# Second mixture of a fused attention and two-mixture kernel: ten weight quarters split ahead of time, kept in DRAM and fetched as parts

## The chip, the cores and the metric

The kernel runs on one core of a Trainium2 chip. The metric is device time in microseconds, the median of several runs. The engines are named as in the profile: PE is TensorE (matmul; PEld its weight loads), DVE is VectorE, ACT is ScalarE, POOL is GpSimd and SP is SyncE, which here only issues DMAs.

## The reference

Three stages follow each other. The third is the one that the change is about; the second is where the work goes.

```python
# 1: a chunked state-space attention over (4, 8 heads, 768, 32) gives x of 3072 tokens x 256
# 2: first mixture, 4 experts, every token through every expert
for e in range(4):
    h = np.maximum(x @ w1[e], 0.0)            # 256 -> 1024
    out += p[:, e:e + 1] * (h @ w2[e])        # 1024 -> 256
# 3: second mixture, 8 experts, each token goes to its best expert alone
expert_idx = np.argmax(x @ w_gate, axis=1)    # tokens gathered by expert into disp
h = np.maximum(np.einsum('ecd,edf->ecf', disp, w1), 0.0)
y = np.einsum('ecf,efd->ecd', h, w2)
out[i] = gate_w[i] * y[expert_idx[i], pos[i]]
```

## The kernel before

**Numbers in two parts.** Every fp32 weight and activation is split into a rounded high part and a low part (`fp32r`), and a product is three matmuls: high by high, high by low, low by high. A split is one ACT copy that makes the high part and one subtraction that makes the low part (`split_w`, L373; the copy is L379, the subtraction L380). Weights come from DRAM in quarters of 128 x 1024 (512 KB): quarters 0 and 1 are the halves of `w1`, quarters 2 and 3 those of `w2`.

**First mixture.** Tokens stand in seven blocks of 2, 3, 4, 4, 4, 4 and 3 times 128. For each block and expert, eight chunks f run: `up` (PE makes `ph`, ACT makes `hh` from it at L509, DVE makes `hl` at L510) and, two chunks later, `down`. Each such step ends in `tick`, which emits what is listed for that slot (`at_slot`), and then a share of the attention of the next block; there are 64 slots in a block of 32 chunks, so slot 2f follows `up` of chunk f. The attention's `mask` (L247) on DVE must be ready before PE's `products` (L255, L263, L291). POOL adds the experts' results (L557).

**Second mixture.** Expert e's tokens are gathered by DMA (`load_rows`, L696), turned on PE (`turn`, L703) and split (`turned`, L711 and L712). A set of branches that `choose` (L1082) makes picks an arm for each expert by its number of tokens: `narrow_program` (up to 256), one wide block (up to 384), or `full_program` (two blocks). Each arm runs `expert_block`: `up_part` makes `qh` on PE (L733 to L735), ACT makes `ring_hh` (L737) and DVE `ring_hl` (L738); `down_part` (L749, L750) adds up `yy`; at the end ACT and DVE scale it (L778, L779) and POOL scatters it to the output (L780). The first three chunks of expert e+1 (`head`; the third goes into a tile named `qs`) are the last thing in expert e's arm. `qh` has two buffers, so `up_part` of chunk 5 needs `ring_hl` of chunk 3 to be done.

**Weights of the second mixture.** Four sets of weight tiles serve eight experts, so set e+2 is filled while expert e runs. All of experts 0 to 2 is split in the last block of the first mixture, on POOL. In the arms of experts 1 to 5, `first_block` splits the four quarters of expert e+2 at slots 4, 6, 8 and 10, with the subtraction on DVE for quarters 1 and 2 and on POOL for 0 and 3; the raw quarter that takes the freed staging tile is loaded three slots later, five places ahead in the list `order`. A slot is a call of `go` in `expert_block`. In a narrow arm slots 1 to 3 come at once, slot 4 stands before chunk 3, and from there two slots belong to each chunk.

```python
        for c in range(4 if e + 2 < E2 else 0):
            m, i = (4, 6, 8, 10)[c], 4 * (e + 2) + c
            add(m, lambda w=order[i], lo=(nc.vector if c in (1, 2) else nc.gpsimd): split_w(2, *w, lo))
```

Each engine executes its own instructions in the order in which the program emits them, and waits at each for the semaphores of the others.

Of the kernel before, what the change touches and what calls it, by code (L numbers as in the profile page):

```python
# [8 lines left out]
F32 = mybir.dt.float32  # L9
F32R = mybir.dt.float32r  # L10
# [3 lines left out]
ALU = mybir.AluOpType  # L14
# [3 lines left out]
P = 128  # L18
# [4 lines left out]
DM = NH * HD  # L23
E1 = 4
E2 = 8
FF = 1024
# [43 lines left out]
def attention_moe_moe_kernel(ctx: ExitStack, tc: tile.TileContext, aps: dict, cap: int):  # L70
    nc = tc.nc
# [8 lines left out]
    sp = ctx.enter_context(tc.tile_pool(name="stage", bufs=3))  # L80
    hp_ = ctx.enter_context(tc.tile_pool(name="hidden", bufs=3))
    dp = ctx.enter_context(tc.tile_pool(name="scratch", bufs=1, space=bass.MemoryType.DRAM))
# [269 lines left out]
    late_pool = []  # L352
    W = {}

    def weight_src(moe, e, c):
        w1, w2 = aps[f"w1_{moe}"][e], aps[f"w2_{moe}"][e]
        if c < 2:
            return w1[P * c:P * c + P, :]
        return w2[512 * (c - 2):512 * (c - 2) + 512, :].rearrange("(f p) d -> p f d", p=P)

    def load_w(moe, e, c):
        if (moe, e, c) not in given:
            pool, n = (late_pool[0], 2) if moe == 2 and (4 * e + c) % 5 > 2 else (sp, 3)
            given[moe, e, c] = pool.tile([P, FF], F32, tag="stage", name=f"stg{moe}_{e}_{c}", bufs=n)
        st = given[moe, e, c]
        nc.sync.dma_start(st if c < 2 else st.rearrange("p (f d) -> p f d", d=DM), weight_src(moe, e, c))
    def weights(moe, e):
        w1 = [wp.tile([P, KD * FF], F32R, tag=n, name=f"{n}_{moe}_{e}") for n in ("w1h", "w1l")]
        w2 = wp.tile([P, 2, KD * FF], F32R, tag="w2", name=f"w2_{moe}_{e}")
        return [*w1, w2[:, 0], w2[:, 1], w2]  # L370


    def split_w(moe, e, c, lo):  # L373
        if (moe, e) not in W:
            W[moe, e] = weights(moe, e)
        h, l = W[moe, e][2 * (c // 2):2 * (c // 2) + 2]
        sl = slice(FF * (c % 2), FF * (c % 2) + FF)
        st = given[moe, e, c]
        nc.scalar.copy(h[:, sl], st)  # L379
        lo.tensor_tensor(l[:, sl], st, h[:, sl].bitcast(F32), ALU.subtract)  # L380
# [313 lines left out]
    def load_rows(e, k):  # L694
        base = e * cap_slots + k * SLOTS
        nc.sync.dma_start(place(e, k), disp[base:base + SLOTS, :].rearrange("(t p) d -> p t d", p=P))  # L696

    def turn(e, k):
        rows = place(e, k)
        t = [ps.tile([P, SLOTS], F32, tag="s", name=f"tr{e}_{k}_{d}", bufs=3) for d in range(KD)]  # L700
        for d in range(KD):
            for st in range(ST):
                nc.tensor.transpose(t[d][:, P * st:P * st + P], rows[:, st, P * d:P * d + P], ident)  # L703
        tp[e, k] = t
        nc.gpsimd.tensor_copy(gi[e, k], rows[:, :, DM:ROW])

    def turned(e, k):
        t = tp.pop((e, k))
        xh, xl = xs[e, k]
        for d in range(KD):  # L710
            nc.scalar.copy(xh[:, d], t[d])  # L711
            nc.vector.tensor_tensor(xl[:, d], t[d], xh[:, d].bitcast(F32), ALU.subtract)  # L712
# [95 lines left out]
    def hint(label):  # L808
        tc.mark_branch_hint_location(label, "LikelyTaken", engines=[mybir.EngineType.PE])
# [63 lines left out]
    for c in range(3):  # L873
        load_w(1, 0, c)
    loaded[2] = [load_decay(2, a_src, nc.sync), None, None, None]
    load_w(1, 0, 3)
    nc.gpsimd.memset(state, 0.0)
    clip_all()
# [21 lines left out]
    for c in range(4):  # L900
        load_w(1, 1, c)
# [14 lines left out]
    def at_slot(b, i, fn):  # L916
        wq.setdefault((b, i), []).append(fn)
# [28 lines left out]
        at_slot(0, i, lambda e=e, c=c: load_w(1, e, c))  # L946
    at_slot(0, 28, gating_loads)
    at_slot(0, 42, gating_setup)
    order = [(e, c) for e in range(E2) for c in range(4)]
    when = [18, 21, 24, 27, 34, 37, 40, 43, 50, 53, 56, 59]  # L950
    split_at(last, when[0:4], 2, 0)
    split_at(last, when[4:8], 2, 1)
# [29 lines left out]
    for i in range(len(seq) + LAG):  # L982
        if i < len(seq):
            b, e, f = seq[i]
# [53 lines left out]
    for i in range(5, len(order)):  # L1038
        e, c = order[i]
# [9 lines left out]
    def first_block(e, n, y, lead, two=False, over=None):  # L1049
        extra = {}  # L1050

        def add(i, fn):
            extra.setdefault(i, []).append(fn)

        if over:
            add(8, lambda: hint(over))
        if two:
            add(1, lambda: load_rows(e, 1))
            add(6, lambda: turn(e, 1))
            add(8, lambda: turned(e, 1))  # L1060
        if e + 1 < E2:
            add(1, lambda: load_rows(e + 1, 0))
            add(10, lambda: turn(e + 1, 0))
            add(12, lambda: turned(e + 1, 0))
        for c in range(4 if e + 2 < E2 else 0):
            m, i = (4, 6, 8, 10)[c], 4 * (e + 2) + c
            add(m, lambda w=order[i], lo=(nc.vector if c in (1, 2) else nc.gpsimd): split_w(2, *w, lo))
            if i + 5 < len(order):
                add(m + 3, lambda w=order[i + 5]: load_w(2, *w))
        expert_block(e, 0, n, extra, HEAD, early=(lead, y))  # L1070

    def second_into(e, tokens):
# [15 lines left out]
    def full_program(e, tokens, y):  # L1088
        first_block(e, SLOTS, y, LEAD, two=True)
        second_into(e, tokens)  # L1090
        head(e + 1)
        if e + 1 < E2:
            align(JOIN)

    def wide_programs(e, tokens, y, after):
        if nblk == 1:
            first_block(e, SLOTS, y, LEAD)
            head(e + 1)
            return
        choose(tokens <= SLOTS, f"full{e}", lambda: first_block(e, SLOTS, y, LEAD, over=f"next{e}"), None)  # L1100
        choose(tokens > SLOTS, f"next{e}", lambda: full_program(e, tokens, y), after)
# [85 lines left out]
```

## Time and profile before

| | |
|---|---|
| median of 3 runs | 780.46 us (779.81 to 781.44) |
| the profiled execution | 778.74 us |
| its span, first to last instruction | 776.9 us |
| granted TensorE clock, mean | 0.998 |
| PE busy | 759.9 us (98%) |
| DVE, ACT, POOL busy | 439.0, 284.4, 187.7 us |
| bytes moved by DMA | 82.52 MB |

The span is divided by the program's stages: the seventh block of the first mixture ends at about 602 us, expert 0 of the second mixture runs to 641 us, and experts 1 to 7 follow up to 771 us. In this data experts 1 and 3 take the wide arm, experts 2, 4, 5 and 6 the narrow one, expert 7 two blocks. Experts 2, 4, 5 and 6 thus run the same PE program, and expert 6 does it without any split beside it.

### The profile page before, as it was taken

The numbers are of one execution on the slowest core, as the hardware profiler recorded it, in microseconds if no ns is written. First come the engines' busy times: TensorE is split into PE (matmuls) and PEld (weight loads), VectorE is DVE, ScalarE is ACT, GpSimd is POOL, SyncE is SP. The second block draws the span as 40 slices with busy tenths as digits, with TensorE's granted clock in tenths as the row PEclk, the third lists the DMA queues.
The fourth block names the chain that finished last, engine by engine and source line by source line (L and its number), as shares of the span: only waits on it lengthen the run. The fifth ranks groups of instructions, "written<-read, shape, count | busy, mean of one in ns | idle before, by whom it ended". The sixth has DMA issues, their size and how long they took to land. (4 is left out here: it accounts for less than half of the span.)

```text
span 776.9 us, 12841 instructions
## 1 busy us (share of the span) xinstructions
PE 759.9 (98%) x4746; PEld 666.3 (86%) x4746; DVE 439.0 (57%) x872; ACT 284.4 (37%) x579; POOL 187.7 (24%) x227
## 2 busy tenths in 40 slices
PE   9999999999999999999999999999999999898996
PEld 7889999987888878888888888889999999797996
DVE  5785788456663576635676456553533545657432
ACT  1553443233332333323332333322444235456431
POOL 1010102212210132110321112111396215544411
PEclk9999999999999999999999999999999999999999
DMA  9763567623210232102322022131154204454000
GB/s 257 234 204 106 188 217 220 180 86 105 82 59 27 85 113 84 69 22 77 114 85 82 17 72 86 41 105 53 51 178 128 94 23 151 159 171 137 27 34 28
DMA packets 50195, 82.52 MB, mean 106 GB/s; under 512 B 5104, under 2 KB 35009, under 8 KB 50108
## 3 DMA queue, kind: packets, MB, share of 16 engines
q1 hardware_dynamic: 46340, 74.50, 30.2%
q0 software_dynamic: 2400, 6.11, 2.2%
q10 hardware_dynamic: 1368, 0.81, 0.5%
q8 instruction: 47, 0.77, 0.4%
q14 instruction: 40, 0.33, 0.1%
HBM read 65.56 MB, written 16.31 MB: 105 GB/s over the span
## 5 line engine op out<-in xcount | busy, mean ns | idle before, releaser
L510 DVE SCALAR_TENSOR_TENSOR hl<-ph,hh 128x512 fp32r<-128x512 f32 (+2 forms) x216 | 133.7, 619 | 232.6 <-ACT hh L509 228.9
L509 ACT ACTIVATE hh<-ph 128x512 fp32r<-128x512 f32 (+2 forms) x216 | 117.2, 543 | 344.0 <-PE ph L506 339.4
L504 PE MATMUL ph<-xh,w1h 128*128 128x512 f32 (+2 forms) x432 | 160.6, 372 | 0.7 <-DVE hl L510 0.7
L533 PE MATMUL acc<-hh,w 128*128 128x512 f32 (+2 forms) x432 | 158.0, 366 | 0.6 <-DVE x L549 0.5
L505 PE MATMUL ph<-xl,w1h 128*128 128x512 f32 (+2 forms) x432 | 156.4, 362 | 0.0
L506 PE MATMUL ph<-xh,w1l 128*128 128x512 f32 (+2 forms) x432 | 156.3, 362 | 0.0
L534 PE MATMUL acc<-hl,w 128*128 128x512 f32 (+2 forms) x432 | 156.3, 362 | 0.0
L535 PE MATMUL acc<-hh,w 128*128 128x512 f32 (+2 forms) x432 | 156.1, 361 | 0.0
L533 PEld LDWEIGHTS acc<-hh,w 128*128 128x128 f32 x432 | 81.2, 188 | 13.0 <-issue 1.4
L504 PEld LDWEIGHTS ph<-xh,w1h 128*128 128x128 f32 x432 | 81.2, 188 | 12.6 <-issue 2.4
L506 PEld LDWEIGHTS ph<-xh,w1l 128*128 128x128 f32 x432 | 81.2, 188 | 10.4
L535 PEld LDWEIGHTS acc<-hh,w 128*128 128x128 f32 x432 | 81.3, 188 | 10.4
L534 PEld LDWEIGHTS acc<-hl,w 128*128 128x128 f32 x432 | 81.3, 188 | 9.4
L505 PEld LDWEIGHTS ph<-xl,w1h 128*128 128x128 f32 x432 | 81.3, 188 | 8.7
L557 POOL TENSOR_TENSOR x<-x,cmb 128x512 f32<-128x512 f32 (+2 forms) x40 | 48.5, 1234 | 153.1 <-DVE cmb L554 153.0
L749 PE MATMUL yy<-w,ring_hh 128*128 128x512 f32 x208 | 76.4, 398 | 0.0
L738 DVE SCALAR_TENSOR_TENSOR ring_hl<-qh,ring_hh 128x384 fp32r<-128x384 f32 (+2 forms) x77 | 36.5, 476 | 55.9 <-ACT ring_hh L737 52.6
L750 PE MATMUL yy<-w,ring_hl 128*128 128x256 f32 x208 | 58.4, 281 | 0.0
L737 ACT ACTIVATE ring_hh<-qh 128x384 fp32r<-128x384 f32 (+2 forms) x77 | 32.9, 427 | 68.4 <-PE qh L735 66.6
L181 DVE TENSOR_TENSOR_SCAN lt<-abc,id 128x512 f32<-128x512 f32 x44 | 57.3, 1303 | 0.0
L733 PE MATMUL qh<-sxh,w1h 128*128 128x256 f32 (+2 forms) x126 | 39.0, 310 | 6.7 <-DVE ring_hl L738 6.4
L749 PEld LDWEIGHTS yy<-w,ring_hh 128*128 128x128 f32 x208 | 39.1, 188 | 6.2
(171 smaller groups left out, 996.1 us busy)
## 6 DMA issues: line engine op xcount, KB each, us to landing
stg<-in_w SPq DMA_DIRECT2D x34, 512.0 KB, 4.3
abc<-a_zero SPq DMA_DIRECT2D x21, 512.0 KB, 3.7
bcr<-in_bc SPq DMA_DIRECT2D x19, 512.0 KB, 3.8
disp<-zrow SPq DMA_DIRECT2D x12, 516.0 KB, 6.6
nat<-in_nat SPq DMA_DIRECT2D x24, 256.0 KB, 4.5
pb<-pT SPq DMA_DIRECT2D x16, 256.0 KB, 4.3
rw<-disp SPq DMA_DIRECT2D x10, 387.0 KB, 4.5
early_w<-in_w SPq DMA_DIRECT2D x6, 512.0 KB
```

The costliest lines, as they stand in the source:

```text
L181: nc.vector.tensor_tensor_scan(t["lt"][:, sl, :].rearrange("p h i -> p (h i)"), a_bc[:, sl, :].rearrange("p h i -> p (h i)"), id4.rearrang ...
L504: nc.tensor.matmul(ph[:, :n], lhsT=wh[:, c], rhs=xh[:, k, :n], start=k == 0, stop=False)
L505: nc.tensor.matmul(ph[:, :n], lhsT=wh[:, c], rhs=xl[:, k, :n], start=False, stop=False)
L506: nc.tensor.matmul(ph[:, :n], lhsT=wl[:, c], rhs=xh[:, k, :n], start=False, stop=k == KD - 1)
L509: nc.scalar.activation(hh[:, :n], ph[:, :n], AF.Relu)
L510: nc.vector.scalar_tensor_tensor(hl[:, :n], ph[:, :n], 0.0, hh[:, :n].bitcast(F32), ALU.max, ALU.subtract)
L533: nc.tensor.matmul(a[:, :n], lhsT=wh[:, c], rhs=hh[:, :n], start=f == 0, stop=False)
L534: nc.tensor.matmul(a[:, :n], lhsT=wh[:, c], rhs=hl[:, :n], start=False, stop=False)
L535: nc.tensor.matmul(a[:, :n], lhsT=wl[:, c], rhs=hh[:, :n], start=False, stop=f == NF - 1)
L557: (nc.vector if (b, e) == (last, experts(b)[-1]) else nc.gpsimd).tensor_tensor(dst[d], dst[d], tmp[d], ALU.add)
L749: nc.tensor.matmul(y, lhsT=hh[:, q], rhs=w2[:, :, c], start=j == 0, stop=False)
L750: nc.tensor.matmul(y[:, 0], lhsT=hl[:, q], rhs=w2[:, 0, c], start=False, stop=j == NF - 1)
```

## The change

Ten quarters (0 and 3 of experts 3 to 7, the list `apart`) are no longer loaded and split in the second mixture. In blocks 2 to 5 of the first mixture, three to a block, each is loaded, split in two halves of 512 columns (ACT copy, DVE subtraction in place) and its two parts are stored to the DRAM tile `parts`. In the arms of experts 1 to 5 four DMAs of 512 KB fetch the two parts of both quarters straight into the weight tiles at slot 2. The other two quarters are split at slots 4 and 7, both on DVE, and the raw loads follow two slots later; `order` now has 22 entries, so only the arms of experts 1, 2 and 3 still load raw quarters (2, 2 and 1 of them).

```diff
+    apart = [(e, c) for e in range(3, E2) for c in (0, 3)]
+    order = [(e, c) for e in range(E2) for c in range(4) if (e, c) not in apart]
+    parts = dp.tile([len(apart), 2, P, FF], F32, name="parts")
+    making = {}
+
+    def part_load(i):
+        making[i] = [sp.tile([P, FF], F32, tag="stage", name=f"raw{i}", bufs=3)]
+        st = making[i][0]
+        c = apart[i][1]
+        nc.sync.dma_start(st if c < 2 else st.rearrange("p (f d) -> p f d", d=DM), weight_src(2, *apart[i]))
+
+    def part_split(i, half):
+        if not half:
+            making[i].append(sp.tile([P, FF], F32R, tag="stage", name=f"high{i}", bufs=3))
+        st, h = making[i]
+        sl = slice(FF // 2 * half, FF // 2 * half + FF // 2)
+        nc.scalar.copy(h[:, sl], st[:, sl])
+        nc.vector.tensor_tensor(st[:, sl].bitcast(F32R), st[:, sl], h[:, sl].bitcast(F32), ALU.subtract)
+
+    def part_store(i):
+        st, h = making.pop(i)
+        nc.sync.dma_start(parts[i, 0], h.bitcast(F32))
+        nc.sync.dma_start(parts[i, 1], st)
+
+    def part_fetch(e, c):
+        sl = slice(FF * (c % 2), FF * (c % 2) + FF)
+        for k, w in enumerate(W[2, e][2 * (c // 2):2 * (c // 2) + 2]):
+            nc.sync.dma_start(w[:, sl].bitcast(F32), parts[apart.index((e, c)), k])
...
-    order = [(e, c) for e in range(E2) for c in range(4)]
+    for i in range(len(apart)):
+        b, s = 2 + i // 3, 16 * (i % 3)
+        at_slot(b, s + 2, lambda i=i: part_load(i))
+        at_slot(b, s + 20, lambda i=i: part_split(i, 0))
+        at_slot(b, s + 24, lambda i=i: part_split(i, 1))
+        at_slot(b, s + 27, lambda i=i: part_store(i))
...
         for c in range(4 if e + 2 < E2 else 0):
-            m, i = (4, 6, 8, 10)[c], 4 * (e + 2) + c
-            add(m, lambda w=order[i], lo=(nc.vector if c in (1, 2) else nc.gpsimd): split_w(2, *w, lo))
+            if (e + 2, c) in apart:
+                add(2, lambda c=c: part_fetch(e + 2, c))
+                continue
+            m, i = 3 * c + 1, order.index((e + 2, c))
+            add(m, lambda w=order[i]: split_w(2, *w, nc.vector))
             if i + 5 < len(order):
-                add(m + 3, lambda w=order[i + 5]: load_w(2, *w))
+                add(m + 2, lambda w=order[i + 5]: load_w(2, *w))
```

PE's instructions stand in the same order in both programs. Three places of the other engines show what moved.

DVE, the narrow arm of expert 2, before (`w1l`, `w` are the low parts of expert 4's weights, `stg` the raw quarters, `qh` chunks 3 to 7):

```order
L738 SCALAR_TENSOR_TENSOR ring_hl_6201<-qh_0_3_7576,ring_hh_6200 128x256
L380 TENSOR_TENSOR w1l_0_5657<-stg_3_0_6002,w1h_0_5656 128x1024
L738 SCALAR_TENSOR_TENSOR ring_hl_6205<-qh_0_4_7591,ring_hh_6204 128x256
L380 TENSOR_TENSOR w_2_0_5658<-stg_3_1_6085,w_2_0_5658 128x1024
L738 SCALAR_TENSOR_TENSOR ring_hl_6209<-qh_0_5_7607,ring_hh_6208 128x256
L738 SCALAR_TENSOR_TENSOR ring_hl_6201<-qh_0_6_7632,ring_hh_6200 128x256
```

The same arm after the change:

```order
L409 TENSOR_TENSOR w1l_0_5748<-stg_4_1_6203,w1h_0_5747 128x1024
L767 SCALAR_TENSOR_TENSOR ring_hl_6292<-qh_0_3_7665,ring_hh_6291 128x256
L767 SCALAR_TENSOR_TENSOR ring_hl_6296<-qh_0_4_7679,ring_hh_6295 128x256
L409 TENSOR_TENSOR w_2_0_5749<-stg_4_2_6235,w_2_0_5749 128x1024
L767 SCALAR_TENSOR_TENSOR ring_hl_6300<-qh_0_5_7694,ring_hh_6299 128x256
L767 SCALAR_TENSOR_TENSOR ring_hl_6292<-qh_0_6_7717,ring_hh_6291 128x256
```

The first subtraction has moved ahead of `ring_hl` of chunk 3; the second still stands ahead of chunk 5. POOL's two subtractions of this arm are gone.

SP, the narrow arm of expert 2, before (`rw` is the gathered rows of expert 3):

```order
L696 DMA rw_6196<-disp 128x3x258
L366 DMA stg_4_0_6169<-in_w_2 128x1024
L366 DMA stg_3_0_6002<-in_w_2 128x4x256
L366 DMA stg_3_1_6085<-in_w_2 128x4x256
L366 DMA stg_3_2_6112<-in_w_2 128x1024
L1082 UNCONDITIONAL_BRANCH x2
```

The same arm after the change:

```order
L725 DMA rw_6287<-disp 128x3x258
L388 DMA w1h_0_5747<-parts 128x1024
L388 DMA w1l_0_5748<-parts 128x1024
L388 DMA w_2_0_5749<-parts 128x1024 x2
L395 DMA stg_4_1_6203<-in_w_2 128x4x256
L395 DMA stg_4_2_6235<-in_w_2 128x1024
L1119 UNCONDITIONAL_BRANCH x2
```

Four fetches now stand behind the rows and ahead of two raw loads.

DVE, end of block 2 of the first mixture, before (`lt` is the attention's decay scan, `m` its masks, `cmb` the product with an expert's probability):

```order
L554 TENSOR_TENSOR cmb_3_1_2659<-acc_3_1_2480,pb_3_2276 128x512
L247 TENSOR_TENSOR m_2663<-sc_0_2648,lt_2635 128x512
L510 SCALAR_TENSOR_TENSOR hl_0_2_2673<-ph_0_2_2665,hh_0_2_2672 128x512
L181 SCALAR_TENSOR_TENSOR lt_2635<-abc_2506,id_87 128x512
L510 SCALAR_TENSOR_TENSOR hl_0_3_2702<-ph_0_3_2694,hh_0_3_2701 128x512
L247 TENSOR_TENSOR m_2705<-sc_1_2679,lt_2635 128x512
L510 SCALAR_TENSOR_TENSOR hl_0_4_2735<-ph_0_4_2727,hh_0_4_2734 128x512
```

The same place after the change:

```order
L583 TENSOR_TENSOR cmb_3_1_2680<-acc_3_1_2497,pb_3_2284 128x512
L247 TENSOR_TENSOR m_2684<-sc_0_2669,lt_2656 128x512
L539 SCALAR_TENSOR_TENSOR hl_0_2_2694<-ph_0_2_2686,hh_0_2_2693 128x512
L378 TENSOR_TENSOR raw_2462<-raw_2462,high_2697 128x512
L181 SCALAR_TENSOR_TENSOR lt_2656<-abc_2523,id_87 128x512
L539 SCALAR_TENSOR_TENSOR hl_0_3_2726<-ph_0_3_2718,hh_0_3_2725 128x512
L247 TENSOR_TENSOR m_2729<-sc_1_2703,lt_2656 128x512
L539 SCALAR_TENSOR_TENSOR hl_0_4_2759<-ph_0_4_2751,hh_0_4_2758 128x512
L378 TENSOR_TENSOR raw_2462<-raw_2462,high_2697 128x512
```

A half subtraction (`raw`) stands ahead of the second decay scan and so ahead of the second mask, and another behind chunk 4's `hl`.

## Rows read from the trace of the kernel before

**Rows 1.** The page's first part: busy time by engine.

```profile
PE 759.9 (98%) x4746; PEld 666.3 (86%) x4746; DVE 439.0 (57%) x872; ACT 284.4 (37%) x579; POOL 187.7 (24%) x227
```

**Rows 2.** Waits of PE, 600 to 777 us: total, times, longest.

```profile
PE qh L733 <- DVE ring_hl L738: 6.4, 5, 2.0
```

**Rows 3.** Timeline, DVE, second mixture: start, duration, instruction, idle before it.

```profile
661.12 0.96 DVE L738 SCALAR_TENSOR_TENSOR ring_hl<-qh,ring_hh 128x256 fp32r<-128x256 f32 x2 [0.37 <-ACT ring_hh L737]
...
668.40 3.35 DVE L380 TENSOR_TENSOR w<-stg,w 128x1024 fp32r<-128x1024 f32 x1
...
676.65 0.96 DVE L738 SCALAR_TENSOR_TENSOR ring_hl<-qh,ring_hh 128x256 fp32r<-128x256 f32 x2 [0.37 <-issue]
...
695.12 0.95 DVE L738 SCALAR_TENSOR_TENSOR ring_hl<-qh,ring_hh 128x256 fp32r<-128x256 f32 x2 [0.37 <-ACT ring_hh L737]
...
711.78 0.96 DVE L738 SCALAR_TENSOR_TENSOR ring_hl<-qh,ring_hh 128x256 fp32r<-128x256 f32 x2 [0.37 <-ACT ring_hh L737]
...
715.68 1.23 DVE L380 TENSOR_TENSOR w1l<-stg,w1h 128x1024 fp32r<-128x1024 f32 x1 [0.51 <-ACT w1h L379]
...
723.85 0.96 DVE L738 SCALAR_TENSOR_TENSOR ring_hl<-qh,ring_hh 128x256 fp32r<-128x256 f32 x2 [0.38 <-ACT ring_hh L737]
...
735.93 0.96 DVE L738 SCALAR_TENSOR_TENSOR ring_hl<-qh,ring_hh 128x256 fp32r<-128x256 f32 x2 [0.38 <-ACT ring_hh L737]
```

**Rows 4.** Timeline, POOL, second mixture.

```profile
668.30 2.37 POOL L380 TENSOR_TENSOR w<-stg,w 128x1024 fp32r<-128x1024 f32 x1
...
717.77 2.87 POOL L380 TENSOR_TENSOR w1l<-stg,w1h 128x1024 fp32r<-128x1024 f32 x1 [4.46 <-DMA rw<-disp]
```

**Rows 5.** Timeline, PE, chunks 5 and 7 of expert 2, chunk 5 of expert 4.

```profile
665.36 0.38 PE L733 MATMUL qh<-sxh,w1h 128*128 128x256 f32 x1
...
672.14 0.39 PE L733 MATMUL qh<-sxh,w1h 128*128 128x256 f32 x1 [1.94 <-DVE ring_hl L738]
...
700.48 0.39 PE L733 MATMUL qh<-sxh,w1h 128*128 128x256 f32 x1 [0.84 <-DVE ring_hl L738]
```

**Rows 6.** Timeline, ACT, third head chunk and first cast of experts 2, 4, 5, 6.

```profile
663.24 0.38 ACT L737 ACTIVATE ring_hh<-qs 128x256 fp32r<-128x256 f32 x1 [1.62 <-PE qs L735]
663.52 1.04 ACT L379 CAST w1h<-stg 128x1024 fp32r<-128x1024 f32 x1
...
698.02 0.39 ACT L737 ACTIVATE ring_hh<-qs 128x256 fp32r<-128x256 f32 x1 [2.40 <-PE qh L735]
698.64 1.05 ACT L379 CAST w1h<-stg 128x1024 fp32r<-128x1024 f32 x1 [0.24 <-issue]
...
713.38 1.05 ACT L379 CAST w1h<-stg 128x1024 fp32r<-128x1024 f32 x1
...
724.64 0.38 ACT L737 ACTIVATE ring_hh<-qs 128x256 fp32r<-128x256 f32 x1 [0.29 <-PE qs L735]
```

**Rows 7.** Groups by line and form, first 600 us: the subtraction of a quarter on DVE.

```profile
L380 DVE TENSOR_TENSOR w1l<-early_w1l,w1h 128x1024 fp32r<-128x1024 f32 x4 | 4.9, 1216 | 0.7 <-ACT w1h L379 0.5
```

**Rows 8.** Waits of PE, 130 to 600 us: the only row.

```profile
PE y L263 <- DVE m L247: 0.2, 1, 0.2
```

**Rows 9.** Timelines of POOL, DVE and PE at the end of block 2.

```profile
227.32 2.56 POOL L557 TENSOR_TENSOR x<-x,cmb 128x512 f32<-128x512 f32 x2 [19.70 <-DVE cmb L554]
...
223.84 1.21 DVE L181 TENSOR_TENSOR_SCAN lt<-abc,id 128x512 f32<-128x512 f32 x1
...
229.56 1.40 DVE L181 TENSOR_TENSOR_SCAN lt<-abc,id 128x512 f32<-128x512 f32 x1
231.94 0.69 DVE L510 SCALAR_TENSOR_TENSOR hl<-ph,hh 128x512 fp32r<-128x512 f32 x1 [0.98 <-ACT hh L509]
...
233.29 0.43 PE L263 MATMUL y<-m,nat 128*32 128x128 f32 x8 [0.19 <-DVE m L247]
```

**Rows 10.** Timeline of SP, expert 2's rows; windows, expert 1's four loads (last: DMA share, GB/s).

```profile
662.52 0.37 SPq L696 DMA_DIRECT2D rw<-disp  x1
...
652.00:660.00 8.00, 8.00 (x52) 7.43 (x51) 5.40 (x10) 4.16 (x9) 3.65 (x3) 1.00 0.77 258
```

More of the change, by code (lines that the diff above doesn't have):

```diff
@@ L359, in weight_src @@
         return w2[512 * (c - 2):512 * (c - 2) + 512, :].rearrange("(f p) d -> p f d", p=P)
+    apart = [(e, c) for e in range(3, E2) for c in (0, 3)]
[22 more added lines that the diff above has]
+            nc.sync.dma_start(w[:, sl].bitcast(F32), parts[apart.index((e, c)), k])
     def load_w(moe, e, c):
         if (moe, e, c) not in given:
-            pool, n = (late_pool[0], 2) if moe == 2 and (4 * e + c) % 5 > 2 else (sp, 3)
+            pool, n = (late_pool[0], 2) if moe == 2 and order.index((e, c)) % 5 > 2 else (sp, 3)
             given[moe, e, c] = pool.tile([P, FF], F32, tag="stage", name=f"stg{moe}_{e}_{c}", bufs=n)
```

## The prediction

> **What bounds the kernel now.** I read the page's first part first. PE is busy for 759.9 us of a span of 776.9 [rows 1], so no change that leaves PE's work alone can gain more than the remaining 17 us, and PE's instructions here stay in the same order. The next view is the list of PE's waits in the second mixture: 6.4 us in five waits, all of chunk matmuls for `ring_hl`, DVE's low part of an earlier chunk [rows 2]. In the middle of the first mixture, from 130 to 600 us, the same view has a single 0.2 us [rows 8]. The second mixture is thus where something can be won, and the first is where something can be lost.
>
> The timeline of DVE tells what the waits cost in all. Experts 2, 4, 5 and 6 run the same narrow PE program, and each begins with the pair of `ring_hl` of its head. From pair to pair expert 6, which splits nothing, takes 735.93 - 723.85 = 12.08 us; expert 5 takes 723.85 - 711.78 = 12.07; expert 2 takes 676.65 - 661.12 = 15.53 and expert 4 takes 711.78 - 695.12 = 16.66 [rows 3]. Experts 2 and 4 therefore lose 3.45 + 4.58 = 8.03 us. The wait list has 6.4 of it; the rest is in matmuls that restart slowly or run beside a missing operand.
>
> Why does expert 5 lose nothing, with the same four splits? Its DVE subtraction took 1.23 us, and POOL began its own only at 717.77, after it; in expert 2 POOL subtracted from 668.30 to 670.67, and DVE's subtraction that began at 668.40 lasted 3.35 us, to 671.75 [rows 3, 4]. Chunk 7 of expert 2 then waited 1.94 us for the `ring_hl` behind it [rows 5]. A quarter's subtraction on DVE with no POOL work beside it takes 1216 ns [rows 7]. So the loss is DVE's subtraction beside POOL's.
>
> **Second mixture: what is removed.** POOL's ten subtractions go, so no DVE subtraction runs beside one, and two of four ACT casts per arm go, 1.04 us each [rows 6]. For the stretch this leaves 1.22 us per subtraction. By that alone the whole 8.03 us would come back.
>
> **What is added there.** The first subtraction now stands ahead of `ring_hl` of chunk 3, and chunk 5 on PE needs that result. ACT casts first, so chunk 3's result is ready at the cast's end, plus 0.05 us to start, 1.22 for the subtraction and about 0.4 for `ring_hl` (a pair takes 0.96 with its gap [rows 3]). The cast begins when ACT has done the third head chunk, and here a row matters that has nothing to do with splits: that activation came 1.62 us late in expert 2 and 2.40 late in expert 4, where expert 6 has 0.29 [rows 6]. If ACT is as late again:
>
> - Expert 2: 663.52 + 1.04 + 0.05 + 1.22 + 0.4 = 666.2. Chunk 5 could start at 665.36 [rows 5, 6]. New wait 0.9 us.
> - Expert 4: 698.64 + 1.05 + 0.05 + 1.22 + 0.4 = 701.4. Chunk 5 started at 700.48 after a wait of 0.84, so it could have started at 699.64 [rows 5, 6]. New wait 1.75 us.
> - Expert 5: 713.38 + 1.05 + 0.05 + 1.22 + 0.4 = 716.1. Expert 2's chunk 5 stood 665.36 - 661.12 = 4.24 us behind its pair; the same offset here gives 711.78 + 4.24 = 716.0 [rows 3, 5, 6]. New wait 0.1 us.
>
> The second subtraction stands ahead of `ring_hl` of chunk 5, as before, has its cast no later than before, and takes 1.22 us where 3.35 us made chunk 7 wait 1.94; 1.94 is less than the 2.1 us saved, so nothing is left. Experts 1 and 3, in the wide arm, show no PE wait now, and PE has 384 columns per chunk to cover the same 1.22 us: nothing. Total: 8.03 - 0.9 - 1.75 - 0.1 = 5.3 us gained.
>
> **The fetches.** Four of 512 KB are 2.1 MB per arm; expert 1's four raw loads moved at 258 GB/s [rows 10], which makes 8.1 us. Expert 2's are issued behind the rows at 662.52 and first needed by expert 4's head just ahead of 695.12 [rows 3, 10], 32 us later; the last, in expert 5's arm, have more than 20. What covers them is the whole of the arm between. All six transfers and the rows are 3.5 MB and 13.7 us, more than a narrow arm of 12.1, but only experts 1 and 2 have six, and the rows that PE turns stand ahead of the fetches in SP's queue. Bounds: nothing, or 13.7 - 12.1 = 1.6 us once, if expert 3's arm finds its rows queued behind expert 2's loads. I take nothing, since expert 3 is wide and turns later.
>
> **First mixture: what is added.** Ten loads, twenty stores, twenty ACT copies and twenty DVE subtractions of 512 columns in blocks 2 to 5. Half of the quarter's price is 0.61 us, a DVE row of 512 columns has 0.69 [rows 7, 9]: 12 to 14 us of DVE in all, about 3.5 us per block. What hides it is DVE's idle time in front of each `hl`. The tightest place I found is the end of block 2: DVE's decay scan of 1.40 us ends at 230.96, then DVE stands idle for 0.98 us until ACT's `hh`, makes `hl`, then the second mask, and PE already waits 0.19 us for that mask [rows 9]. The new half stands ahead of the scan. 0.69 of the 0.98 us idle are used, and the mask is not later. If the cover were missing, the mask and PE would be late by the full 0.69 us. The same place comes back in blocks 3 and 4, so the bounds are 0 and 3 x 0.69 = 2.1 us. Elsewhere PE waits for neither masks nor `hl` today [rows 8]. I take 0.1 us. Stores and loads wait for work that was emitted slots before; ACT's copy of 0.52 us goes behind `hh`, where it delays only itself.
>
> POOL's adds at that place run until 227.32 + 2.56 = 229.88, and the half would begin at 229.56 [rows 9]. If it only shared with POOL, it would stretch as the scan did, 1.40 us against 1.21 for the scan before it, which had no POOL add beside it [rows 9]; if it had to wait for POOL's end, it would begin 0.32 late and end at 230.5 instead of 230.2, and a scan of 1.21 would end at 231.75, before 231.94. Both give nothing on the path. The Trainium skill (SBUF — State Buffer, section "Who interferes with whom") says that a DVE instruction with two SBUF inputs contends with a GpSimd instruction that reads SBUF, and that the loser blocks for the whole instruction; by that rule each half that meets a POOL add is late, and the sum is still unchanged as long as 0.98 us of idle time covers it.
>
> **Sum.** The profiled execution took 778.74 us, 1.7 us less than the median of the runs shown. 778.74 - 5.3 + 0.1 = 773.5. The same 5.2 us off the median of 780.46 give 775.3 us, a gain of 0.67%. A measurement of this kernel can tell about 0.2%, 1.6 us, from no change.
>
> **Rivals.**
>
> *ScalarE's lateness is not there.* It came in experts 2 and 4, both behind a wide arm, and not in expert 6. If it stays away, the three waits of 2.75 us vanish and the gain is 8.0: 772.4 us. Against it: nothing in the change is meant to touch it. Chance 0.18.
>
> *The lateness grows or spreads.* ACT was late by 1.62 and 2.40 us with no POOL or DVE work to wait for [rows 6]. If the new bursts of 2.1 MB at the start of each arm make ACT 1 us later in the three narrow arms, each us goes straight into chunk 5's wait, since the new order left no slack there: 3 us less gain, 778.3 us. Above 1.2 us each the change is lost in the noise. Chance 0.10. The Trainium skill (Runtime: NRT & Kernel Launch, section "Instruction fetch mechanics") says that a taken branch whose target lies outside the loaded window must fetch instructions by DMA before it goes on. By that rule the lateness is an instruction load, the new program has its pages elsewhere, and either this rival or the one before it would come true; no row here shows such a load as the cause.
>
> *Another wait takes the gain.* The rows or the fetches come late at two or three arms (1.6 us each by the bound above), and the time stays within 0.2%: 780 us. Against it, 32 us of cover. Chance 0.06.
>
> *Slower: the first mixture pays.* DVE's halves delay masks or `hl`. Each of the twenty costs at most 0.69 us, 13.8 us in all: 775.2 + 13.8 = 789 us. It decides from the point where they cost more than 5.2 + 1.6 = 6.8 us, so where at least ten of twenty come through. Against it: 0.2 us of PE waits in 470 us and DVE idle in front of nearly every `hl`; for it: a mask that PE waits for even now. Chance 0.06.
>
> **How the numbers follow.** My forecast, ACT as late as now, has 0.60 and a range of its own from 774 to 777 (half the lateness more or less, and the 2.1 us bound of the first mixture). 772.0 to 778.4 takes in the first two rivals and leaves out the last two, 0.12, and a little at the edges. Faster by over 0.2%: 0.60 + 0.18 + 0.10 = 0.88; within 0.2%: 0.06; slower: 0.06.
>
> **What would show it.** In the profile after: no POOL subtraction of 128x1024 behind 605 us; DVE's at 1.2 us each; expert 6's pair-to-pair time still 12.1 us, experts 2 and 4 at about 13 and 14; PE waits for `ring_hl` of 2 to 3 us, all at chunk 5; PE's waits from 130 to 600 us still under 0.5 us. I am wrong if PE waits for a DMA of `parts`, if masks in blocks 2 to 4 make PE wait by half a microsecond each, or if experts 2 and 4 stay above 15 us with short subtractions, which would say that ACT and not POOL made them late.

## The result, and the profile after

The changed kernel takes 770.79 us (median, 769.0 to 772.34) and the kernel before, beside it on the same chip, 780.13 (777.52 to 781.44): a ratio of 0.9879, 95% interval 0.9856 to 0.9901. I had said 775.3, with a range down to 772.0. The sign was right, the gain was 9.3 us in place of 5.2, and the time lies 1.2 us below the range. The profiled execution took 771.84 us, so from profile to profile the gain is 6.9 us.

The page's first part, to be held against [rows 1]:

```profile
PE 759.5 (99%) x4746; PEld 666.5 (87%) x4746; DVE 444.6 (58%) x892; ACT 286.3 (37%) x589; POOL 159.3 (21%) x217
```

PE's work is the same; 6.8 us of the span around it have gone. Waits of PE, first from 600 to 771 us, then from 130 to 600 us (total, times, longest):

```profile
PE qh L762 <- PEq L1119: 0.3, 1, 0.3
...
PE y L263 <- DVE m L247: 0.2, 1, 0.2
```

The 6.4 us for `ring_hl` of [rows 2] are gone, and the first mixture waits as before [rows 8]. The timeline of DVE, with the head pairs of experts 1 to 7 and the two subtractions of expert 2, answers to [rows 3]:

```profile
643.01 0.97 DVE L767 SCALAR_TENSOR_TENSOR ring_hl<-qh,ring_hh 128x256 fp32r<-128x256 f32 x2 [0.37 <-ACT ring_hh L766]
...
661.57 0.95 DVE L767 SCALAR_TENSOR_TENSOR ring_hl<-qh,ring_hh 128x256 fp32r<-128x256 f32 x2 [0.38 <-ACT ring_hh L766]
...
664.29 1.23 DVE L409 TENSOR_TENSOR w1l<-stg,w1h 128x1024 fp32r<-128x1024 f32 x1 [0.51 <-ACT w1h L408]
...
666.65 1.23 DVE L409 TENSOR_TENSOR w<-stg,w 128x1024 fp32r<-128x1024 f32 x1 [0.46 <-ACT w L408]
...
673.92 0.96 DVE L767 SCALAR_TENSOR_TENSOR ring_hl<-qh,ring_hh 128x256 fp32r<-128x256 f32 x2 [0.41 <-ACT ring_hh L766]
...
692.50 0.96 DVE L767 SCALAR_TENSOR_TENSOR ring_hl<-qh,ring_hh 128x256 fp32r<-128x256 f32 x2 [0.37 <-ACT ring_hh L766]
...
704.95 0.96 DVE L767 SCALAR_TENSOR_TENSOR ring_hl<-qh,ring_hh 128x256 fp32r<-128x256 f32 x2 [0.43 <-issue]
...
717.04 0.96 DVE L767 SCALAR_TENSOR_TENSOR ring_hl<-qh,ring_hh 128x256 fp32r<-128x256 f32 x2 [0.41 <-ACT ring_hh L766]
...
729.12 0.96 DVE L767 SCALAR_TENSOR_TENSOR ring_hl<-qh,ring_hh 128x256 fp32r<-128x256 f32 x2 [0.37 <-ACT ring_hh L766]
```

From pair to pair expert 2 takes 12.35 us (15.53 before), expert 4 12.45 (16.66), experts 5 and 6 12.09 and 12.08 as before. Of the 8.03 us lost, 0.64 are left, where I had put 2.75; no wait at chunk 5 is long enough for the list. The row behind that is ACT's third head chunk, in experts 2 and 4, to be held against 1.62 and 2.40 us in [rows 6]:

```profile
662.93 0.39 ACT L766 ACTIVATE ring_hh<-qs 128x256 fp32r<-128x256 f32 x1 [0.88 <-PE qs L764]
...
693.90 0.39 ACT L766 ACTIVATE ring_hh<-qs 128x256 fp32r<-128x256 f32 x1 [0.90 <-PE qs L764]
```

A head that nothing holds up shows 0.28 us there. I call the excess its lateness: 1.34 and 2.12 us before, 0.60 and 0.62 after. (My prediction called the whole idle time late, and passed over expert 5, whose third head chunk was 0.53 us late before.)

### The profile page after: what moved, and what is told of

The parts are those of the page before. It is cut to its first block, busy times and chain, and to the rows that moved or that the text cites. A ratio compares the mean times of both kernels' runs of the same rounds, so it can differ in the third digit from the quotient of the medians.

```text
span 770.1 us, 12919 instructions
## 1 busy us (share of the span) xinstructions
PE 759.5 (99%) x4746; PEld 666.5 (87%) x4746; DVE 444.6 (58%) x892; ACT 286.3 (37%) x589; POOL 159.3 (21%) x217
## 5 line engine op out<-in xcount | busy, mean ns | idle before, releaser
L809 POOL DMA_INDIRECT out<-yo,gi x26 | 25.5, 979 | 78.6 <-DVE yo L808 75.1
```

## The experiments

The runs came in sets, each on one chip (I call them A to F; A is that of the result), with the kernel before beside them. That kernel takes 780 us on some chips and 771 on others, so the chip belongs to every number. Lateness is the time from the end of the second head activation to the start of the third, less 0.28 us. Executions also differ by some 2.4 us in their first 15 us (`slots_late` and `slots_again` stood at the same DVE instruction at 12.51 and 14.96 us and kept the distance). The column "from expert 1" leaves that out: the span less the start of expert 1's head pair. Arms, lateness and this column are of the one profiled execution, the median is of all; "before there" is the median of the kernel before in the same set.

| run | chip | median us | before there | arms 2, 4 us | lateness 2, 4 us | from expert 1 |
|---|---|---|---|---|---|---|
| before | A | 780.13 | | 15.5, 16.7 | 1.34, 2.12 | 134.2 |
| the change | A | 770.79 | 780.13 | 12.35, 12.45 | 0.60, 0.62 | 127.1 |
| after_pool | B | 775.58 | 781.12 | 13.9, 14.2 | 2.17, 1.52 | 130.8 |
| before_dve | B | 772.18 | 781.12 | 12.9, 14.1 | 0.22, 1.49 | 129.7 |
| before_make | B | 778.44 | 781.12 | 15.6, 15.7 | 0.80, 1.43 | 133.4 |
| after_slots | B | 769.69 | 781.12 | 12.1, 12.1 | 0.68, 1.41 | 126.1 |
| after_again | C | 770.43 | 771.07 | 12.1, 12.1 | 0, 0 | 126.6 |
| after_act0 | C | 773.59 | 771.07 | 12.1, 12.1 | 0, 0 | 126.6 |
| after_act128 | C | 770.27 | 771.07 | 12.1, 12.1 | 0, 0 | 126.5 |
| before_dve_later | C | 775.14 | 771.07 | 13.6, 13.6 | 0, 0 | 132.2 |
| before_again | D | 771.25 | 771.32 | 12.1, 12.4 | 0, 0 | 126.4 |
| after_late | D | 774.17 | 771.32 | 13.4, 13.4 | 1.64, 1.64 | 129.1 |
| slots_late | D | 769.95 | 771.32 | 12.1, 12.1 | 1.64, 1.64 | 126.3 |
| slots_again | D | 768.97 | 771.32 | 12.1, 12.1 | 0, 0 | 126.2 |
| before_late | E | 780.17 | 781.12 | 16.4, 16.5 | 2.17, 1.64 | 134.9 |
| before_late_one | E | 781.58 | 781.12 | 17.9, 18.3 | 2.17, 1.56 | 139.7 |
| before_late_half | E | 781.19 | 781.12 | 16.4, 16.7 | 1.55, 1.54 | 135.1 |
| late_pool_last | E | 777.17 | 781.12 | 14.3, 14.5 | 1.64, 1.64 | 132.1 |
| before_late_b | F | 781.09 | 780.51 | 16.4, 18.0 | 2.15, 1.64 | 136.4 |
| before_late_half_b | F | 780.98 | 780.51 | 15.65, 18.25 | 1.46, 2.17 | 135.8 |

**GpSimd's subtractions put back (`after_pool`).** In `first_block` of the changed kernel:

```diff
             add(m, lambda w=order[i]: split_w(2, *w, nc.vector))
+            if c == 1:
+                add(m, lambda w=order[i]: twice(*w))
...
+    def twice(e, c):
+        h = W[2, e][0][:, FF:2 * FF].bitcast(F32)
+        for _ in range(2):
+            nc.gpsimd.tensor_tensor(scratch, given[2, e, c], h, ALU.subtract)
```

> The changed kernel, and GpSimd makes the subtraction of quarter 1 twice more in each of the arms of experts 1 to 5, into a scratch tile that nobody reads. Theory 1 (VectorE's subtraction is held up by a GpSimd subtraction that runs beside it): VectorE's second subtraction of an arm, which starts some 2.4 us behind the first, grows from 1.23 us to between 2 and 3.4, the pair-to-pair time of experts 2 and 4 rises from 12.4 to 13.5 to 14.5 us, that of expert 5 from 12.1 likewise, waits of chunk matmuls for the low parts come back with 3 to 6 us in all, and the time is 774 to 777 us. Theory 2 (the gain came from halving the number of splits in an arm, and GpSimd's share of them did not matter): nothing changes, 769 to 772 us.

775.58 us, a ratio of 0.9932 (0.9912 to 0.9952) to the kernel before. DVE's second subtraction of expert 2 was held up as theory 1 says. But the wait on PE stands elsewhere; DVE, then PE, expert 2:

```profile
665.94 1.23 DVE L409 TENSOR_TENSOR w1l<-stg,w1h 128x1024 fp32r<-128x1024 f32 x1 [0.51 <-ACT w1h L408]
...
667.75 2.74 DVE L409 TENSOR_TENSOR w<-stg,w 128x1024 fp32r<-128x1024 f32 x1
```

```profile
667.55 0.39 PE L762 MATMUL qh<-sxh,w1h 128*128 128x256 f32 x1 [1.34 <-DVE ring_hl L767]
```

PE's wait ends at 667.55, before the long subtraction begins: it is chunk 5 waiting for the low part of chunk 3, behind a head that was 2.17 us late. Expert 4 shows the same, with 1.47 us. So the time that theory 1 forecast came about by lateness, which is luck, and the stretch of 1.5 us cost little: the list has no wait at chunk 7 of either arm. The run shows the hold-up, not its price.

**One word in the kernel before (`before_dve`).** `lo=nc.vector` for all four subtractions of an arm, nothing split ahead:

> The kernel before with one word changed: all four subtractions of an arm are VectorE's, at the old slots, with nothing split ahead and nothing fetched. Theory 1: every subtraction takes 1.2 us, experts 2 and 4 come down from 15.5 and 16.7 us to between 12.5 and 14.5, as ScalarE's lateness and four times 1.6 us of VectorE work per arm against 1.43 us per chunk of TensorE leave some wait, and the time is 774 to 776.5 us. Theory 2: all four splits are still there and the time stays at 778 to 780.5 us.

772.18 us, ratio 0.9882 (0.9858 to 0.9907): about what the whole change won on chip A, and below the range of theory 1. All 20 subtractions take 1.21 to 1.23 us. Theory 2 falls. What is left sits in expert 4, with a head 1.49 us late and a subtraction ahead of `ring_hl` of chunk 3; PE, chunk 5:

```profile
699.11 0.39 PE L733 MATMUL qh<-sxh,w1h 128*128 128x256 f32 x1 [1.21 <-DVE ring_hl L738]
```

**The first mixture by itself (`before_make`).** The kernel before with the load, split and store pieces of the change, and no fetch.

> The kernel before, and the ten quarters are also loaded, split and stored in the first mixture as in the change, but never fetched: the price of the first mixture by itself. My sum took 0.1 us: the time stays within 0.5 us of the kernel before, TensorE's waits between 130 and 600 us stay under 0.5 us. The rival that the first mixture pays: 0.3 us (the shift seen at the start of expert 1 after the change) up to 13.8 us more.

778.44 us, ratio 0.9965 (0.9946 to 0.9984): not slower, and PE waits 0.2 us there as before. It is 2.7 us faster, where I expected at most 0.5 of difference; I put that down to smaller lateness in its executions (the profile's is 0.80 and 1.43), which is argued only. At the place of [rows 9], DVE, then PE:

```profile
230.01 0.84 DVE L377 TENSOR_TENSOR raw<-raw,high 128x512 fp32r<-128x512 f32 x1
230.77 1.21 DVE L181 TENSOR_TENSOR_SCAN lt<-abc,id 128x512 f32<-128x512 f32 x1
```

```profile
233.70 0.43 PE L263 MATMUL y<-m,nat 128*32 128x128 f32 x8 [0.18 <-DVE m L247]
```

The half meets POOL's add and takes 0.84 us (0.68 is the median of the twenty in the changed kernel), the scan behind it 1.21 instead of 1.40, and the mask makes PE wait 0.18 us (0.19 before).

**The old slots (`after_slots`).** The changed kernel with `m = 2 * c + 4` and the loads at `m + 3`.

> The changed kernel with the two splits of an arm at slots 6 and 8, where the kernel before had VectorE's two, in place of 4 and 7, and the loads three slots later as before. My prediction held the new order, a subtraction ahead of the low part of chunk 3, for the cause of a wait at chunk 5. If that wait is only there when ScalarE is late at the head, and it is late by no more than 0.6 us now, moving it gives back at most 0.6 us: 770 to 772 us. If the new slots were where the gain came from, experts 2 and 4 rise to 13 us or more, 772 to 774 us.

769.69 us, ratio 0.9852 (0.983 to 0.9874). Expert 4's head was 1.41 us late, and the arm took 12.12 us all the same.

**The same program once more, and two other places for ScalarE's code (`after_again`, `after_act0`, `after_act128`).** The last two put `nc.scalar.addr_align(256, offset=0 or 128, max_nops=0)` at the start of the second mixture.

> The changed kernel once more, nothing edited, for a second profile. ScalarE's lateness at the third head chunk was 0.60 us (expert 2) and 0.62 us (expert 4) in its first profile, 1.34 and 2.12 in the kernel before. Theory L1 (the lateness belongs to the program, by where its instructions lie): the same heads are late by the same amounts within 0.1 us. Theory L2 (it differs from execution to execution): they differ by more than 0.3 us, and where one of them is late by 1.5 us or more, chunk 5 of that expert waits for the low part of chunk 3 by about the lateness less 0.6 us, as the prediction worked it out.

> The changed kernel, with ScalarE's instructions from the start of the second mixture moved to the start of a 256-instruction block (padding that is jumped over; no work changes). Theory L1: the lateness at the heads of experts 2 and 4 moves by more than 0.5 us, to other heads or to none, and by the same amounts in every execution: between 769 us (none late) and 774 (two late by 2 us, each of which makes chunk 5 wait). Theory L2 or no instruction load behind it: lateness between 0.2 and 2.2 us at the same two heads as in all the kernels so far, 769.5 to 772.5 us.

> The same, with ScalarE's instructions half a block further on (offset 128 of 256). Theory L1: another lateness than at offset 0, by more than 0.5 us at one head at least. Theory L2: as at offset 0, within what executions differ.

No head was late in any of these profiles, so L1 falls as it stood (the same program was 0.60 us late on chip A and 0 here), and the code's place could not be tested. And the kernel before took 771.07 us there: the change is worth nothing on this chip (after_again: 0.9991, 0.9975 to 1.0008). The 773.59 of offset 0 (1.0034, 1.0016 to 1.0051) comes with 770.52 in its profiled execution and arms as quick as the others'; its cause stays open.

**All on VectorE, one slot later (`before_dve_later`).** Slots (5, 7, 9, 11) in the one-word version.

> The kernel before with all four subtractions on VectorE, as in the run before, but one slot later (5, 7, 9, 11), so that the low part of chunk 3 stands ahead of the first subtraction. In that run chunk 5 of expert 4 waited 1.21 us behind a head that came 1.49 us late, with a subtraction of 1.23 us ahead of the low part of chunk 3. If the order makes that wait, it is gone or under 0.3 us even with a head 1.5 us late, and the time is 770 to 771.5 us, within 0.2% of the changed kernel: the parts in DRAM would then be worth nothing beyond the order. If the parts are needed for their own sake (ScalarE's and VectorE's work halved), it stays at 772 us or above.

775.14 us, slower than the kernel before there (1.0077, 1.0052 to 1.0102). The order behind chunk 3 is mended and the end spoilt: the fourth subtraction now stands ahead of `sxl` and chunk 7's low part. PE, expert 2:

```profile
671.06 0.39 PE L750 MATMUL yy<-w,ring_hl 128*128 128x256 f32 x1 [0.98 <-DVE ring_hl L738]
```

So halving DVE's work per arm does have a worth: with two subtractions the old slots have a place for both, with four neither place that I tried was free. The one-word version lost 0.86 us in expert 2, whose head was only 0.22 us late; on a chip without late heads it was not run.

**The kernel before, unedited (`before_again`).**

> The kernel before once more, nothing edited. If ScalarE's lateness at the heads of experts 2 and 4 (1.34 and 2.12 us in its first profile) is the program's, it is there again. If it differs from execution to execution or from chip to chip, as the changed kernel's two profiles (0.60 and 0.62 us, then 0.00 and 0.00) say, it can be anything from 0 to 2.2. The loss that VectorE's subtraction beside GpSimd's makes must be there all the same: 2.3 and 3.4 us for the two subtractions of experts 2 and 4, both above 14 us from pair to pair, and a time of 777 to 782 us.

771.25 us: the last sentence of the expectation is wrong. Expert 2 on ACT, DVE and POOL:

```profile
662.26 0.39 ACT L737 ACTIVATE ring_hh<-qs 128x256 fp32r<-128x256 f32 x1 [0.28 <-PE qs L735]
...
661.48 0.96 DVE L738 SCALAR_TENSOR_TENSOR ring_hl<-qh,ring_hh 128x256 fp32r<-128x256 f32 x2 [0.37 <-ACT ring_hh L737]
...
665.15 2.01 DVE L380 TENSOR_TENSOR w1l<-stg,w1h 128x1024 fp32r<-128x1024 f32 x1 [0.51 <-DMA rw<-disp]
...
667.42 1.21 DVE L380 TENSOR_TENSOR w<-stg,w 128x1024 fp32r<-128x1024 f32 x1
...
673.57 0.96 DVE L738 SCALAR_TENSOR_TENSOR ring_hl<-qh,ring_hh 128x256 fp32r<-128x256 f32 x2 [0.38 <-ACT ring_hh L737]
...
663.67 2.40 POOL L380 TENSOR_TENSOR w1l<-stg,w1h 128x1024 fp32r<-128x1024 f32 x1
668.05 2.85 POOL L380 TENSOR_TENSOR w<-stg,w 128x1024 fp32r<-128x1024 f32 x1 [0.57 <-ACT w L379]
```

The head is not late. DVE's first subtraction meets POOL's and takes 2.01 us, which PE doesn't feel. The second starts 0.63 us before POOL's second and takes 1.21; it is POOL's that is stretched, to 2.85, and nobody waits for it. In [rows 3, 4] DVE's second began 0.10 us after POOL's and took 3.35. The arm takes 12.09 us.

**Lateness made by hand (`after_late`; `slots_late` and, without it, `slots_again`).** In `head`, for experts 2 and 4, ahead of the third chunk:

```diff
+            if e in (2, 4) and f == HEAD - 1:
+                for _ in range(2):
+                    nc.scalar.copy(idle[0], W[2, e][0][:, 0:FF].bitcast(F32))
             up_part(e, 0, f, 0, NARROW, f == HEAD - 1)
```

> The changed kernel, and ScalarE makes two copies of 128x1024 that nobody reads (2.1 us) ahead of the third head chunk's activation of experts 2 and 4: a lateness of 1.8 us made by hand, about what the kernel before showed (1.34 and 2.12). My forecast's step (the subtraction now ahead of the low part of chunk 3 makes chunk 5 wait when ScalarE is late): experts 2 and 4 each take 13.2 to 14 us from pair to pair in place of 12.1, with a wait at chunk 5 of 1.2 to 1.7 us each, and the time is 2.4 to 3.6 us above the changed kernel with no lateness: 772 to 774 us. Rival (the new order does not matter, lateness is absorbed): 12.1 to 12.4 us, 769 to 771.5 us.

> The same two copies in the version with the splits at slots 6 and 8, where the low part of chunk 3 stands ahead of the first subtraction and no cast stands ahead of its high part. If the order is what turns lateness into a wait: 12.1 to 12.6 us for experts 2 and 4, no wait above 0.4 us, 769 to 771 us. If any lateness of that size costs its time: 13.2 us or more, 772 to 774 us.

With the change's slots, ACT and then PE of expert 2:

```profile
662.30 2.12 ACT L776 CAST idle<-w1h 128x1024 bf16<-128x1024 f32 x2
664.33 0.38 ACT L766 ACTIVATE ring_hh<-qs 128x256 fp32r<-128x256 f32 x1
```

```profile
667.29 0.39 PE L762 MATMUL qh<-sxh,w1h 128*128 128x256 f32 x1 [1.00 <-DVE ring_hl L767]
```

Each arm takes 13.4 us, 1.25 more than with no lateness (12.12 in `after_again`), and the kernel 774.17 (1.0033, 1.0018 to 1.0049, against the kernel before there). With the old slots the same 1.64 us cost nothing: 12.1 us, no wait for `ring_hl`, 769.95, on the same chip. So the new order is what turns lateness into time.

> The version with the splits at slots 6 and 8 once more, beside the others on one chip, since it was the fastest so far (769.69 us). If it is faster than the changed kernel only where ScalarE is late, it is within 0.2% of it here when no head is late, 769 to 771 us.

768.97 us, ratio 0.998 (0.9969 to 0.9991) to the kernel before there. This version was below the kernel before on both chips, and its stretch from expert 1 on (126.1 to 126.3) was never above the changed kernel's (126.5 to 127.1); the two were not run on one chip.

**Is lateness the trigger of the 8 us?** The copies in the kernel before, in three sizes (`before_late`, `before_late_one`, `before_late_half`), and once two copies with its last split at slot 13 (`late_pool_last`).

> The kernel before, and ScalarE makes two copies of 128x1024 that nobody reads (2.1 us) ahead of the third head chunk's activation of experts 2 and 4, so that this activation is 1.8 us late. The kernel before takes 771 us where no head is late and 780 where those two are. Theory T (lateness is the trigger: ScalarE catches up, its fourth cast comes closer behind its third, GpSimd's second subtraction then starts ahead of VectorE's second and VectorE's is held up): VectorE's second subtraction of experts 2 and 4 goes from 1.2 to 3.3 us, both arms from 12.1 and 12.4 us to 15 to 17, and the time from 771 to 777 to 780 us, 0.8 to 1.2% more than the kernel before on the same chip. Theory U (780 and 771 differ by something else of the chip, and the lateness only goes with it): the lateness costs at most its own 1.8 us twice, 771 to 775 us.

> The same with one copy (0.76 us late). With no head late, VectorE's second subtraction started 0.63 us ahead of GpSimd's in expert 2 (667.42 against 668.05) and 0.28 us ahead in expert 4 (698.34 against 698.62). If theory T holds and the catching up is worth up to 0.77 us (four casts in 4.68 us when late, in 5.45 when not), this lateness is about enough: both experts flip, 776 to 779 us, or expert 4 alone, 774 to 776 us. Theory U: at most 1.5 us more than the kernel before.

> The same with half a copy (about 0.3 us late). Theory T: expert 2 keeps VectorE first (0.63 us ahead); expert 4 is at its edge (0.28 us). Within 0.5 us of the kernel before on the same chip if neither flips, 3 to 4.5 us more if expert 4 does. Theory U: within 0.6 us.

> The kernel before with the two copies (1.8 us late), and the last split of an arm (GpSimd's second) at slot 13 in place of 10, its raw load with it at slot 15: VectorE's second subtraction is then always ahead of GpSimd's second. Theory T: it takes 1.2 us again, both arms come to 12.1 to 13.2 us, and the time is 771 to 773 us for all the lateness. Theory U: as the run with two copies and the old slots.

The chip was one where the heads are late anyway: with half a copy, good for about 0.3 us, they were 1.55 and 1.54 late. 780.17, 781.58 and 781.19 us against 781.12 say nothing new, except that lateness and the order of the two engines go together once more. POOL and DVE, expert 2 of the first of them:

```profile
667.24 2.38 POOL L380 TENSOR_TENSOR w<-stg,w 128x1024 fp32r<-128x1024 f32 x1
```

```profile
667.32 3.38 DVE L380 TENSOR_TENSOR w<-stg,w 128x1024 fp32r<-128x1024 f32 x1
```

The fourth run does tell something: with POOL's second split moved back, DVE's second subtraction is short with the head 1.64 us late. DVE, expert 2:

```profile
666.61 2.92 DVE L380 TENSOR_TENSOR w1l<-stg,w1h 128x1024 fp32r<-128x1024 f32 x1 [0.51 <-ACT w1h L379]
...
669.78 1.21 DVE L380 TENSOR_TENSOR w<-stg,w 128x1024 fp32r<-128x1024 f32 x1
```

777.17 us, ratio 0.9944 (0.9922 to 0.9966), short of the 771 to 773 expected, as the first subtraction is still held up and a new wait of 1.9 us for the gathered rows appears:

```profile
PE tr L703 <- DMA rw<-disp: 1.9, 2, 1.0
PE qh L733 <- DVE ring_hl L738: 1.9, 5, 0.7
```

> The kernel before with ScalarE 1.8 us late by hand at the heads of experts 2 and 4, once more, since the first try fell on a chip where these heads are late anyway (the kernel before 781 us there). It tells the theories apart only where the kernel before takes 771 us. There, theory T: VectorE's second subtraction of experts 2 and 4 takes 3.3 us, and the time is 777 to 780 us. Theory U: 771 to 775 us. Where the kernel before takes 780 us, nothing new: 779 to 781 us.

> The same with half a copy, about 0.3 us late, for the same reason. Where the kernel before takes 771 us, theory T: expert 2 keeps VectorE first (it was 0.63 us ahead), expert 4 is at its edge (0.28 us ahead): 771 to 772 us if neither flips, 774 to 776 us if expert 4 does. Theory U: within 0.6 us of the kernel before.

781.09 and 780.98 us against 780.51: chip F has late heads as well, so neither decides. That lateness by itself flips the order on a chip without it was not seen.

## Why the prediction was wrong

Two steps failed: the size of the wait at chunk 5, and taking the profile's gain off the median as it stood.

**The cause: right.** The loss was DVE's subtraction beside POOL's, shown by the one-word edit. It was both subtractions, not the second alone. Beside the 1.94 of [rows 5], PE waited at chunk 6 of expert 2 and at chunks 6 and 7 of expert 4 of the kernel before:

```profile
668.53 0.38 PE L733 MATMUL qh<-sxh,w1h 128*128 128x256 f32 x1 [0.83 <-DVE ring_hl L738]
...
703.62 0.39 PE L733 MATMUL qh<-sxh,w1h 128*128 128x256 f32 x1 [0.80 <-DVE ring_hl L738]
...
707.27 0.38 PE L733 MATMUL qh<-sxh,w1h 128*128 128x256 f32 x1 [1.96 <-DVE ring_hl L738]
```

Chunk 6 stood behind DVE's first subtraction, which took 2.33 and 2.30 us beside POOL's first (in `before_again`, with no late head, 2.01 and 2.32 cost nothing). Only the 0.84 at chunk 5 of expert 4 [rows 5] stands behind the late head alone. With short subtractions 7.39 of the 8.03 us came back.

**The wait at chunk 5: right in kind, wrong in size; this step failed.** "If ACT is as late again" priced it at 0.9 + 1.75 + 0.1 = 2.75 us. The working holds: the lateness less about 0.4 us, and made by hand, 1.64 us of it cost 1.25 per arm. But the lateness was 0.60 and 0.62 us, and the arms took 0.27 + 0.37 = 0.64 us more than expert 6's; chunk 5 began 4.34 and 4.41 us behind its pair, and 4.19 where no head was late (`after_again`). I had taken one execution's lateness for a property of the program. It runs from 0 to 2.2 us over chips and executions. The rival "ScalarE's lateness is not there" had 0.18 and, with 772.4, came nearest; the lateness was less, not gone, so part of that is luck.

**The sum, profile to profile.** 5.2 predicted, 6.9 measured: 2.1 more from chunk 5 and the 0.1 that I had taken off for the first mixture, less 0.30 us by which expert 1's head pair came later (643.01 against 642.71; 0.27 of it are there at the same DVE instruction at 14.34 and 14.61 us, long before block 2, where the change begins) and 0.26 us in the two wide arms (18.56 and 18.58 us against 18.41 and 18.47), which I had at nothing.

**The median: the step that took the time out of the range.** Of the 4.5 us between 775.3 and 770.79, 1.7 lie between the profiles (773.5 forecast, 771.84 measured) and 2.8 in the way from there to the median; chunk 5 sized as measured would have given 773.2, inside the range. Taking the same 5.2 us off the median supposed that executions differ by a constant. The profile of before was 1.4 us below its median on this chip, that of after 1.05 above: 2.4 us of the 9.3 lie there. The 1.05 fit the start: the changed kernel's executions stand in two groups, 769.0 to 769.73 and 771.84 to 772.34, and the profiled one is of the slower. The 1.4 do not, since before's profile started late too (expert 1's pair at 642.71; an early start puts it near 640.8). It rather lost little behind the start. Of the seven profiles with late heads named below, which take 133.4 to 139.7 us from expert 1 on, its 134.2 is the second shortest. What the median execution lost, and where, no profile shows.

**What I didn't see at all.** The sentence that ACT's late row "has nothing to do with splits". In the seven traces of the kernel before, of before_make and of the versions with copies at the old slots, all with late heads, POOL's second subtraction starts 0.06 to 0.10 us ahead of DVE's in experts 2 and 4; in the one without, DVE's is 0.63 and 0.28 us ahead. The rows give a reason. In expert 2 DVE's first subtraction ends 1.1 us after POOL's first, and DVE's second starts 3.75 us after the start of POOL's first, in either case (664.65 to 668.40 in the kernel before, 663.67 to 667.42 without lateness). POOL's second waits for ACT's fourth cast. Behind a late head the four casts start 1.2 us apart (663.52 to 667.16), and POOL's second follows its first by 3.65 us, just ahead of DVE's; where ACT waits for chunks between the casts they start 1.4 to 1.5 us apart (662.55 to 666.93), and it follows by 4.38 us, behind DVE's. POOL's first, expert 2 of the kernel before:

```profile
664.65 2.41 POOL L380 TENSOR_TENSOR w1l<-stg,w1h 128x1024 fp32r<-128x1024 f32 x1 [1.36 <-ACT w1h L379]
```

The 8 us then need both, a late head and POOL's subtractions; the change takes away the second. This reading is argued from the traces: no run made the heads of the kernel before late on a chip where they are not. What makes a head late stays open.

**The rest held.** No PE wait for `parts`; from 648 to 652 us, where expert 1's fetches run, all DMA together moved 406 GB/s. The first mixture costs 0.03 us (the shift of 0.27 us at its start is 0.30 at its end), against 0.1 taken, and the rival that it pays is out.

The corners, each from one profile and not all from one chip, as time lost in experts 2 and 4 against 12.08 us each: the kernel before, 8.0 us with its heads late and 0.3 without; the change, 2.6 (late by hand) and 0.1; the change with the old slots, 0.05 and 0.1.

## What to carry to other kernels

Before a wait is priced from a trace, ask whether the row behind it is a property of the program: run the unchanged kernel on another chip first, since a loss of 1% here was there in four of the six sets and missing in two. Where two engines hold each other up, look at which one starts first and by how much; 0.1 us one way or 0.3 to 0.6 the other went with some 4 us per arm. And try the smallest edit first: moving the subtractions to one engine gave 0.9882 on one chip where the whole change gave 0.9879 on another. It is no full stand-in: its variant one slot later was 0.8% slower than the kernel before on a chip without late heads, where the changed kernel stayed level.

## What the hardware showed

A DVE subtraction of 128x1024 from SBUF ended 1.08 us after the GpSimd subtraction that began before it (670.67 and 671.75 in [rows 3, 4]), whether it had started 0.10 us behind it, as there, or 1.16 (the first ones of that arm, 664.65 to 667.06 and 665.81 to 668.14). Alone it takes 1.21 us, so it looks as if it waits for the other's end and then runs nearly whole. Where DVE began first, it took 1.21 us and GpSimd 2.85 in place of 2.40. The Trainium skill (SBUF — State Buffer, section "Who interferes with whom") says that the order of issue and not the shape decides who blocks; these rows agree.

ScalarE's head was late by 0.2 to 2.2 us in experts 2 and 4 on chips A and B (in some profiles expert 3 or 5 too, by 0.5), and on E and F beyond what the small copies explain; in the profiles from C and D it was late only where the copies made it so. The Trainium skill (Runtime: NRT & Kernel Launch, section "Instruction fetch mechanics") says that a taken branch whose target lies outside the loaded window waits for its instructions to be fetched. Moving ScalarE's code changed no lateness here, since that chip had none to change. The packets of the instruction queues do not settle it either: one runs from 693.42 to 693.73, just ahead of the changed kernel's late activation at 693.90, but none between 661.29 and 663.24, where the kernel before waits 1.34 us too long. So no run bears it out or rules it out.
